# Shifted copies by packed 64-bit adds on GpSimd, and five small operations moved from GpSimd to VectorE

## The chip, the core and the metric

The kernel runs on one core of a Trainium2 chip. A core has engines that run their own instruction streams side by side and meet at semaphores: TensorE (PE; matrix products, which land in PSUM), ScalarE (ACT; functions such as exp), VectorE (DVE; arithmetic along the free axis), GpSimd (POOL; arithmetic between SBUF tensors) and SyncE (SP; issues DMAs). The time is that of one execution on the device, in microseconds (us). 0.2% of this kernel's time is 2.9 us.

## What is computed

Two transformer layers over 2048 tokens of width 512, 32 heads of 16, and an MLP of width 1792. Both layers use the same weights.

```python
def _layernorm(x, axis=-1, eps=1e-5):
    m = jnp.mean(x, axis=axis, keepdims=True)
    v = jnp.var(x, axis=axis, keepdims=True)
    return (x - m) / jnp.sqrt(v + eps)
...
        scores = jnp.einsum("bhqd,bhkd->bhqk", q, k) * (Dh ** -0.5)
        p = _softmax(scores, axis=-1)
        o = jnp.einsum("bhqk,bhkd->bhqd", p, v)
        return (lambda x, *d: x.transpose(*d))(o, 0, 2, 1, 3).reshape(B, S, D) @ wo
...
        h = jnp.einsum("bsd,df->bsf", x, w1) + b1
        h = _gelu(h)
        return jnp.einsum("bsf,fd->bsd", h, w2) + b2
...
    x = x + _A_ref(_layernorm(x, axis=-1), A_wqkv, A_wo)
    x = x + _B_ref(_layernorm(x, axis=-1), B_w1, B_b1, B_w2, B_b2)
    x = x + _A_ref(_layernorm(x, axis=-1), A_wqkv, A_wo)
    x = x + _B_ref(_layernorm(x, axis=-1), B_w1, B_b1, B_w2, B_b2)
```

## The kernel before

**Cells and passes.** The scores of attention are cut into cells of 128 keys by 512 queries of one head (or 256 queries of two heads in the last segments). A pass is one query segment, one group of heads and a range of key tiles; `passes` lists them in order, and a full pass has 16 key tiles by 4 row groups, 64 cells. There are 4096 cells in all. A score matmul uses 32 rows of the PE array, so up to four cells of different row groups run at once (line 1520).

**Two ways through a cell.** An A cell goes to ScalarE: one `activation` takes the exp of two or three cells from PSUM to SBUF (line 2124), and each needs one product with V (17 columns: 16 values and a column of ones that sums the weights). A D cell goes to VectorE. `dfirst` (line 1785) computes `score * E_SCALE + E_BIAS` into uint16; read as bf16, these bits are a piecewise linear approximation of exp. `dchain` then makes three more copies of the plane, shifted by 32, 64 and 96 (128 would be one octave), and the products of the four planes with V and with copies of V scaled by 0.84, 0.71 and 0.59 (`VW`) are summed, so that the errors of the approximation largely cancel. So a D cell needs four products where an A cell needs one. Which key tiles may be D cells is fixed by `KD`: summed over the passes, 1320 of the 4096. A D cell that VectorE has not taken by the end of its pass goes to ScalarE like any other (`next_act`).

**The copies.** Two D cells make a pair (128 x 1024). The first shift, `one` (line 1944), makes plane 1 out of plane 0, on GpSimd where its planned clock is at most `PSHIFT` = 3 us ahead of VectorE's. The second, `two` (line 1969), makes planes 2 and 3 out of 0 and 1 in one VectorE instruction of 128 x 2048; where GpSimd has room it is split into `more` (line 1978, plane 2, GpSimd) and `far` (line 1976, plane 3, VectorE). Scaled copies of V are made by `vcopies` on GpSimd (line 1449), the masked copy of Q for a pass by `qpad` on GpSimd (line 1468; three buffers), the application of the layer norm by `apply` (line 814; GpSimd, or VectorE at the two ends of the kernel), `rstd` by a power on GpSimd (line 800), and the scaling by the softmax sum in `norm` (line 1021; GpSimd for the first six groups of a segment of 512).

**The order.** Nothing is scheduled at run time. `_Sched` simulates the engines while the program is built: each operation is an `_Op` with an engine and a price in us, generators (threads) yield them in order of their data, and at each step the operation that can start first is put at the end of its engine's stream, by priority among those that are ready. Buffers are pools that threads acquire and release. When a group of scores is placed, `attach`, `trade` and `swap` decide from the planned clocks whether D cells join it, and `solo` places a D cell alone. So a price sets not only when work is due but which engine gets it. The planner also keeps GpSimd and VectorE apart where it marks an operation as `port`: a marked VectorE operation is not planned to start inside a GpSimd operation, and a GpSimd operation gives way to a marked one (`GRACE`, `CLOSE`) or waits for it by a semaphore (`op.lock`). When PE would sit idle for longer than a matmul, `fill` puts in a matmul on constants (line 1508); columns that a round of products has no cell for get one too (line 2199).

**Thresholds by piece.** The thresholds of these decisions (`SWAP`, `TOL`, `TAIL` and thirty more, `NAMES`) are read from `ROWS`, 45 rows of values. The cells are divided into 100 pieces, and `PIECES` names for each piece the row that `turn` installs.

Of the kernel before, what the change touches and what calls it, by code (L numbers as in the profile page):

```python
# [9 lines left out]
F16 = mybir.dt.float16  # L10
U16 = mybir.dt.uint16

D = 512
# [113 lines left out]
)  # L127
PIECES = (34, 25, 0, 23, 19, 41, 43, 12, 5, 5, 0, 21, 1, 44, 11, 35, 13, 13, 5, 19, 36, 44, 44, 40, 44, 22, 0, 8, 15, 24, 27, 0, 0, 0, 10, 0, 0, 35,
          14, 0, 0, 32, 18, 31, 38, 0, 22, 22, 22, 30, 0, 29, 14, 16, 16, 40, 0, 6, 44, 39, 26, 0, 4, 30, 16, 0, 23, 19, 0, 42, 44, 15, 15, 23, 23, 0,
          22, 0, 33, 0, 3, 0, 0, 35, 7, 0, 9, 28, 17, 2, 37, 0, 28, 17, 20, 0, 0, 33, 0, 22)  # L130
CLOSE = 0.35
# [6 lines left out]
PMORE = 1  # L138
# [149 lines left out]

# [271 lines left out]
def bass_interleave_layers__mha_block__dense_activation_gelu__prompt_kernel(  # L560
# [15 lines left out]
    with ExitStack() as es:  # L576
# [46 lines left out]
        T["IDENT"] = sb([128, 128], BF16, "ident")  # L623
        T["NHALF"] = sb([128, 4], F32, "nhalf")
# [46 lines left out]
class _Plan:  # L671
# [12 lines left out]
    def init(self):  # L684
# [97 lines left out]
    def ln(self, tiles, dst, dkeys, prio, quick=False, gate=None):  # L782
# [4 lines left out]
        for t in tiles:  # L787
# [3 lines left out]
            if key[0] == "B":  # L791
# [5 lines left out]
        mvk = ["MV.%d" % t for t in tiles]  # L797
        yield _Op("dve", 0.16, lambda e: e.tensor_scalar(T["VARR"][:, sl], T["MV"][:, sl, 1], 1e-5, None, op0=ALU.add),
                  reads=mvk, writes=["VARR.%d" % c])
        yield _Op("pool", 0.37 + 0.18 * n, lambda e: e.tensor_tensor(  # L800
            out=T["RSTD"][:, sl], in0=T["VARR"][:, sl], in1=T["NHALF"][:, 0:n], op=ALU.pow),
            reads=["VARR.%d" % c, "NHALF"], writes=["RSTD.%d" % c])
        yield _Op("dve", 0.157, lambda e: e.scalar_tensor_tensor(
# [7 lines left out]
    def apply(self, c, t, x, quick):  # L811
        T = self.T
        eng, cost = ("dve", 0.4) if quick else ("pool", 0.77)
        return _Op(eng, cost, lambda e: e.tensor_scalar(
            T["XLN"][:, x, :], T["X"][:, t % XT, :], T["RSTD"][:, t:t + 1], T["NMR"][:, t:t + 1], op0=ALU.mult, op1=ALU.add),
            reads=["X.%d" % (t % XT), "RSTD.%d" % c, "NMR.%d" % c], writes=["XLN.%d" % x])
# [165 lines left out]
    def norm(self, l, seg, g, b, part, final):  # L982
# [33 lines left out]
        o = gb % 2  # L1016
        pool = g < 6 and seg[2] == 512
        nb = w // 32
        for i, t in enumerate(ts):
            o3 = T["OTT"][:, o, 0:w].rearrange("p (k c) -> p k c", c=32)[:, :, 16 * t:16 * t + 16]  # L1020
            yield _Op(*(("pool", 0.63 * w / 512) if pool else ("dve", 0.153 + 0.262 * w / 512)), lambda e, i=i, o3=o3: e.tensor_tensor(
                out=o3, in0=x3[:, i * nb:i * nb + nb, 0:16],
                in1=T["RC"][:, i * nb:i * nb + nb, None].to_broadcast([128, nb, 16]), op=ALU.mult),
                reads=["XT", "RC"], writes=["OTT.%d.%d" % (o, t)])
# [405 lines left out]
    def vcopies(self):  # L1430
# [4 lines left out]
        for v in range(len(first)):  # L1435
            l, seg, g, kts = self.pas[first[v]][:4]
            kd = self.kd(first[v])
            js = list(range(len(kd)))
            if js:
                if used[v % 2] is not None:  # L1440
                    yield ("cond", lambda pi=first[used[v % 2] + 1]: self.pv >= pi)
                used[v % 2] = v
                for j in js:
                    yield ("need", ("V", l, kd[j], kd[j] // 4))
                step = kd[1] - kd[0] if len(kd) > 1 else 1
                gb = self.heads(seg, g)[0]
                src = T["V"][l][:, kd[0]:kd[-1] + 1:step, 8 * gb:8 * gb + 8, :].rearrange("p k h c -> p k (h c)")
                for i, w in enumerate(VW):
                    yield _Op("pool", 0.15 + 0.133 * len(js), lambda e, i=i, w=w, v=v, js=js, src=src: e.tensor_scalar(  # L1449
                        T["VC"][:, v % 2, i, js[0]:js[-1] + 1, :], src, w, 1.0, op0=ALU.mult, op1=ALU.mult),  # L1450
                        reads=["V%d.%d" % (l, kt) for kt in kd] + [self.vone(l, kt) for kt in kd], writes=["VC.%d.%d" % (v % 2, i)])
            yield ("give", ("vc", v))
            if not js:
                continue
            self.lend = 1

    def qpad(self):
        T = self.T
        for pi, (l, seg, g, kts, part, final) in enumerate(self.pas):
# [7 lines left out]
            for i, t in enumerate(ts):  # L1467
                yield _Op("pool", 0.27 + 0.42 * w / 512, lambda e, s=s, q=q, i=i, t=t, w=w: e.tensor_scalar(  # L1468
                    T["QP"][:, s, w * i:w * i + w], q, T["MASK"][:, t:t + 1], 1.0, op0=ALU.mult, op1=ALU.mult),
                    reads=["Q.%d.%d" % (b, qc), "MASK"], writes=["QP.%d" % s])  # L1470
# [448 lines left out]
    def dchain(self, pair):  # L1919
# [20 lines left out]
        key = [[self.dkey(pair, i, j) for j in range(n)] for i in range(2)]  # L1940
        u0, u1 = self.planes(pair, 0, n), self.planes(pair, 1, n)
        if self.s.clock["pool"] <= self.s.clock["dve"] + PSHIFT and len(pair["cells"]) == n:
            a, b = u0.rearrange("p j q -> p (j q)"), u1.rearrange("p j q -> p (j q)")
            one = _Op("pool", 0.15 + 0.45 * n, lambda e, a=a, b=b: e.tensor_scalar(b, a, float(SHIFT), 1.0, op0=ALU.add, op1=ALU.mult),  # L1944
                      reads=key[0], writes=key[1])
        else:
            one = _Op("dve", 0.151 + 0.134 * n, lambda e: e.tensor_scalar(u1, u0, SHIFT, None, op0=ALU.add),
                      reads=key[0], writes=key[1])
        one.port = True
        prio = (lambda: UPRIO if any(c[0] <= self.pv and self.left[c[0]] <= URGENT for c in cells) else CPRIO) if URGENT else None  # L1950
        one.prio = prio
        yield one
# [16 lines left out]
        two = _Op("dve", 0.152 + 0.266 * n, lambda e: e.tensor_scalar(  # L1969
            self.planes(sw, 2, n, True), self.planes(sw, 0, n, True), 2 * SHIFT, None, op0=ALU.add),  # L1970
            reads=key[0] + key[1], writes=key[2] + key[3])
        two.port = True
        two.prio = prio
        if one.eng == "pool" and self.s.clock["pool"] <= self.s.clock["dve"] + PMORE and self.room() >= DUMORE:
            a, c, d, b = u0.rearrange("p j q -> p (j q)"), self.planes(pair, 2, n).rearrange("p j q -> p (j q)"), self.planes(pair, 3, n), u1
            far = _Op("dve", 0.151 + 0.134 * n, lambda e: e.tensor_scalar(d, b, 2 * SHIFT, None, op0=ALU.add),
                      reads=key[1], writes=key[3])
            more = _Op("pool", 0.15 + 0.45 * n, lambda e, a=a, c=c: e.tensor_scalar(c, a, float(2 * SHIFT), 1.0, op0=ALU.add, op1=ALU.mult),  # L1978
                       reads=key[0], writes=key[2])
            far.port = more.port = True  # L1980
            far.prio = more.prio = prio
            yield more
            yield far
        else:
            yield two
        if own:
# [3 lines left out]
        for i in range(2 * EARLYP, 4):  # L1990
            self.products(pair, i)

    def units(self, n):
# [313 lines left out]
```

## Time and profile before

| | |
|---|---|
| median of 3 runs | 1451.74 us (1451.57 to 1451.89) |
| profiled execution | span 1450.5 us, first to last instruction; its page gives no other time |
| engines' busy time | PE 1418.4, ACT 1424.3, DVE 1382.8, POOL 995.5 us |
| granted TensorE clock | 1.000 over the span |
| DMA | 55 GB/s in the mean, 19.4% of 16 engines' time |

The granted clock is full, and so it takes no part in what follows. Busy time is the union of the instructions' intervals; on ACT and DVE an instruction's interval overlaps the next one's by some tens to a hundred ns, so that busy time doesn't show very short waits. A row of the groups of instructions has: line, engine, operation, output<-input, shapes, count, then the busy time in us, the mean ns of one, and the idle time of the engine just before them with what ended it. A row of the timeline has the start in us, the length in us, the engine and the instructions.

### The profile page before, as it was taken

What the parts mean: (1) busy time and instruction counts of PE and PEld (TensorE: products, weight loads), DVE (VectorE), ACT (ScalarE), POOL (GpSimd) and SP (SyncE); (2) the same over time, 40 slices, a digit from 0 to 9 for tenths busy, and PEclk for the clock granted to TensorE, in tenths of its full rate; (3) what the DMA queues carried; (4) which work ended last, traced back from release to release, by engine and by line L of the source; (5) the groups of instructions that cost most, each with busy time, mean ns of one, the idle gap of its engine ahead of it and who ended that gap; (6) DMA issues with size and microseconds to landing.
All of it is one profiled execution on the core that took longest, in us unless ns stands there. A gap on an engine that the chain in (4) does not pass through costs nothing.

```text
span 1450.5 us, 45848 instructions
## 1 busy us (share of the span) xinstructions
PE 1418.4 (98%) x19662; PEld 424.7 (29%) x19662; DVE 1382.8 (95%) x2438; ACT 1424.3 (98%) x1406; POOL 995.5 (69%) x1082
## 2 busy tenths in 40 slices
PE   8999999999999999999999999999999999999999
PEld 3222222222222222222222222222222222344445
DVE  7999999999999999999999999999999999999994
ACT  7999999999999999999999999999999999999996
POOL 6676676767776677777676677687767777667751
PEclk9999999999999999999999999999999999999999
DMA  5100001113221133112431123101132203311021
GB/s 159 47 2 2 2 2 38 38 51 97 60 53 31 58 97 89 45 45 72 106 74 38 60 72 91 45 12 36 38 89 67 67 23 96 118 32 39 17 66 41
DMA packets 122166, 80.29 MB, mean 55 GB/s; under 512 B 36717, under 2 KB 120942, under 8 KB 121966
## 3 DMA queue, kind: packets, MB, share of 16 engines
q1 hardware_dynamic: 121966, 77.36, 19.4%
q8 instruction: 158, 2.59, 0.8%
q14 instruction: 42, 0.34, 0.1%
HBM read 65.54 MB, written 4.19 MB: 48 GB/s over the span
## 4 chain that ended last, share of the span: by engine, by line
ACT 42%; PE 41%; DVE 16%; issue 1%; POOL 0%; DMA 0%; DVEq 0%
ACT pt L2124 36%; PE ps L2191 14%; PE ps L1520 14%; PE ps L681 12%; DVE dp L1785 6%; DVE dp L1969 3%; ACT g L1209 2%; ACT kt L2124 1%; DVE g L1188 1%; DVE kt L1785 1%; PE ps L1508 1%; DVE stats L790 1%; ACT q L2124 1%; DVE v L1785 1%; DVE xt L1011 0%
## 5 line engine op out<-in xcount | busy, mean ns | idle before, releaser
L2124 ACT ACTIVATE pt<-ps 128x1024 bf16<-128x1024 f32 (+1 forms) x1264 | 1265.5, 1136 | 4.9 <-PE ps L1520 3.2
L1785 DVE TENSOR_SCALAR dp<-ps 128x512 uint16<-128x512 f32 x931 | 611.5, 681 | 21.5 <-PE ps L1520 18.2
L1944 POOL TENSOR_SCALAR dp<-dp 128x1024 uint16<-128x1024 uint16 (+1 forms) x468 | 490.1, 1056 | 191.0 <-DVE dp L1969 116.7
L1520 PE MATMUL ps<-qp,kt 32*128 32x512 bf16 x4096 | 558.1, 384 | 15.0 <-ACT pt L2124 7.0
L2191 PE MATMUL ps<-dp,vc 128*17 128x512 bf16 (+1 forms) x3120 | 390.2, 359 | 2.3 <-DVE dp L1969 0.9
L2191 PE MATMUL ps<-pt,v 128*17 128x512 bf16 (+1 forms) x3078 | 379.4, 357 | 0.7 <-DVE dp L1969 0.3
L1520 PEld LDWEIGHTS ps<-qp,kt 32*128 32x128 bf16 x4096 | 141.2, 91 | 576.2 <-ACT pt L2124 197.4
L1969 DVE TENSOR_SCALAR dp<-dp 128x2048 uint16<-128x2048 uint16 (+1 forms) x385 | 272.3, 726 | 3.7 <-POOL dp L1944 3.3
L2191 PE MATMUL ps<-dp,v 128*17 128x512 bf16 (+1 forms) x1040 | 149.5, 359 | 3.1 <-DVE xt L1011 1.6
L681 PE MATMUL ps<-xf,wr 128*32 128x512 bf16 (+1 forms) x1888 | 131.7, 365 | 0.4 <-DVE g L1188 0.2
L2191 PEld LDWEIGHTS ps<-dp,vc 128*17 128x17 bf16 x3120 | 98.0, 88 | 102.0 <-issue 58.6
L2191 PEld LDWEIGHTS ps<-pt,v 128*17 128x17 bf16 x3078 | 96.5, 88 | 76.2 <-issue 44.7
L1449 POOL TENSOR_SCALAR vc<-v 128x680 bf16<-128x680 bf16 (+3 forms) x138 | 90.8, 658 | 38.9 <-DVE dp L1969 18.0
L1785 DVE TENSOR_SCALAR kt<-ps 128x512 uint16<-128x512 f32 x154 | 103.6, 682 | 5.1 <-PE ps L1520 4.4
L681 PE MATMUL ps<-wr,g 128*32 128x512 bf16 x1408 | 105.5, 383 | 0.6 <-DVE dp L1785 0.5
L1944 POOL TENSOR_SCALAR kt<-kt 128x1024 uint16<-128x1024 uint16 x77 | 82.1, 1068 | 32.4 <-DVE dp L1969 26.9
L1468 POOL TENSOR_SCALAR qp<-q,mask 128x512 bf16<-128x512 bf16 (+1 forms) x91 | 63.7, 700 | 58.5 <-DVE dp L1969 22.3
L1978 POOL TENSOR_SCALAR dp<-dp 128x1024 uint16<-128x1024 uint16 x83 | 86.6, 1044 | 10.2 <-DVE dp L1969 4.3
L2191 PE MATMUL ps<-kt,vc 128*17 128x512 bf16 (+1 forms) x582 | 88.6, 337 | 0.3 <-DVE kt L1969 0.2
L1188 DVE TENSOR_SCALAR g<-ps,hb1t 128x512 bf16<-128x512 f32 (+1 forms) x112 | 79.3, 708 | 0.7 <-PE ps L681 0.5
L2199 PE MATMUL ps<-b2row,zero 128*17 128x512 bf16 x369 | 78.5, 381 | 0.0
L2191 PE MATMUL ps<-kt,v 128*17 128x512 bf16 (+1 forms) x277 | 57.6, 350 | 0.9 <-DVE dp L1969 0.6
(112 smaller groups left out, 1416.4 us busy)
## 6 DMA issues: line engine op xcount, KB each, us to landing
wr<-in_B_w_dram SPq DMA_DIRECT2D x174, 256.0 KB, 2.9
wr<-in_A_wqkv_dram SPq DMA_DIRECT2D x24, 256.0 KB, 3.1
x<-in_A_x_dram SPq DMA_DIRECT2D x7, 512.0 KB, 4.2
wr<-in_A_wo_dram SPq DMA_DIRECT2D x10, 256.0 KB, 2.9
kept<-x SPq DMA_DIRECT2D x4, 512.0 KB, 2.9
x<-kept SPq DMA_DIRECT2D x4, 512.0 KB, 4.0
out_dram<-x SPq DMA_DIRECT2D x16, 128.0 KB, 1.9
q<-in_B_w_dram SPq DMA_DIRECT2D x3, 512.0 KB, 6.3
```

What stands on the lines that cost most here:

```text
L681: return [lambda e, a=a: e.matmul(out[32 * a:32 * a + 32, :], lhsT=lhsT[:, 32 * a:32 * a + 32], rhs=rhs, start=start, stop=stop, tile_posi ...
L1188: yield _Op("dve", 0.21 + n / 966, lambda e, fc=fc, pb=pb: e.tensor_scalar(T["G"][:, fc, q], pb, T["HB1T"][:, fc:fc + 1], None, op0=ALU.ad ...
L1449: yield _Op("pool", 0.15 + 0.133 * len(js), lambda e, i=i, w=w, v=v, js=js, src=src: e.tensor_scalar(T["VC"][:, v % 2, i, js[0]:js[-1] + 1 ...
L1468: yield _Op("pool", 0.27 + 0.42 * w / 512, lambda e, s=s, q=q, i=i, t=t, w=w: e.tensor_scalar(T["QP"][:, s, w * i:w * i + w], q, T["MASK"] ...
L1520: return (lambda e: e.matmul(o, lhsT=lhsT, rhs=rhs, start=True, stop=True, tile_position=(32 * a, 0)), ["K%d.%d.%d" % (l, gb, kt // 4), "Q ...
L1785: yield _Op("dve", 0.682, lambda e: e.tensor_scalar(u, self.bank(b), E_SCALE, E_BIAS, op0=ALU.mult, op1=ALU.add), reads=["B.%d" % b], writ ...
L1944: one = _Op("pool", 0.15 + 0.45 * n, lambda e, a=a, b=b: e.tensor_scalar(b, a, float(SHIFT), 1.0, op0=ALU.add, op1=ALU.mult), reads=key[0] ...
L1969: two = _Op("dve", 0.152 + 0.266 * n, lambda e: e.tensor_scalar(self.planes(sw, 2, n, True), self.planes(sw, 0, n, True), 2 * SHIFT, None, ...
L1978: more = _Op("pool", 0.15 + 0.45 * n, lambda e, a=a, c=c: e.tensor_scalar(c, a, float(2 * SHIFT), 1.0, op0=ALU.add, op1=ALU.mult), reads=k ...
L2124: yield _Op("act", 0.065 + 0.4267 * n, lambda e, src=src, dst=dst: e.activation(out=dst, in_=src, func=ACT.Exp, scale=0.25), reads=["B.%d" ...
L2191: op.fns.append(lambda e, o=o, lhsT=q[0][0][m], rhs=q[0][1][:, n * m:n * m + n], a=a, st=st, sp=sp: e.matmul(o, lhsT=lhsT, rhs=rhs, start= ...
L2199: op.fns.append(lambda e, o=self.bank(b)[32 * a:32 * a + 17, :], rhs=rhs, a=a, st=not begun[a], sp=end: e.matmul(o, lhsT=T["ZERO"][:, 0:17 ...
```

## The change

1. Shifted copies: `shift` makes both `one` and `two`. On GpSimd it reads four uint16 as one 64-bit integer and adds `by * 32` to each by one `int64_add` with a constant (no value overflows its 16 bits). `one` is 256 words per partition for a pair, `two` 512. `one` goes to GpSimd under the same condition as before; `two` goes there where GpSimd's planned clock is at most `PMORE` = 1 us ahead of VectorE's, else to VectorE as before. The split into `more` and `far` is gone.
2. Five operations go to VectorE: the scaled copies of V, the masked copies of Q, all applications of the layer norm, all scalings by the softmax sum, and `rstd`, which becomes an integer estimate of the inverse root and two correction steps: one power on GpSimd becomes six more VectorE instructions.
3. The planner marks these VectorE operations as `port`, and prices the packed add at 0.18 us and 0.0017 us per word.
4. All 100 pieces use row 0 of `ROWS`.

`KD`, the passes, the priorities and the buffers stay.

```diff
-PIECES = (34, 25, 0, 23, 19, 41, 43, 12, 5, 5, 0, 21, 1, 44, 11, 35, 13, 13, 5, 19, 36, 44, 44, 40, 44, 22, 0, 8, 15, 24, 27, 0, 0, 0, 10, 0, 0, 35,
...
+PIECES = (0,) * 100
...
+PFIX = 0.18
+PWORD = 0.0017
...
+PACKED = SHIFT * 0x0001000100010001
...
+PORTS = ("OTT", "NMR", "RSTD", "RA.", "RY.", "XLN", "VC", "QP")
...
-        self.port = eng == "dve" and self.writes[:1] != [] and self.writes[0].startswith(("OTT", "NMR"))
+        self.port = eng == "dve" and self.writes[:1] != [] and self.writes[0].startswith(PORTS) and not any(k.startswith("B.") for k in self.reads)
...
-        yield _Op("pool", 0.37 + 0.18 * n, lambda e: e.tensor_tensor(
-            out=T["RSTD"][:, sl], in0=T["VARR"][:, sl], in1=T["NHALF"][:, 0:n], op=ALU.pow),
...
+        yield _Op("dve", 0.16, lambda e: e.tensor_scalar(y.bitcast(I32), v.bitcast(I32), -0.5, R_MAGIC, op0=ALU.mult, op1=ALU.add),
+                  reads=vk, writes=yk)
+        for i, (by, less) in enumerate(((1.0, R_LESS), (R_BY * R_BY, 3.0))):
+            yield _Op("dve", 0.16, lambda e: e.tensor_tensor(out=a, in0=y, in1=y, op=ALU.mult), reads=yk, writes=ak)
...
-        eng, cost = ("dve", 0.4) if quick else ("pool", 0.77)
-        return _Op(eng, cost, lambda e: e.tensor_scalar(
+        return _Op("dve", 0.41, lambda e: e.tensor_scalar(
...
-        pool = g < 6 and seg[2] == 512
...
-                    yield _Op("pool", 0.15 + 0.133 * len(js), lambda e, i=i, w=w, v=v, js=js, src=src: e.tensor_scalar(
+                    yield _Op("dve", 0.151 + 0.036 * len(js), lambda e, i=i, w=w, v=v, js=js, src=src: e.tensor_scalar(
...
-                yield _Op("pool", 0.27 + 0.42 * w / 512, lambda e, s=s, q=q, i=i, t=t, w=w: e.tensor_scalar(
+                yield _Op("dve", 0.21 + 0.134 * w / 512, lambda e, s=s, q=q, i=i, t=t, w=w: e.tensor_scalar(
...
+        yield self.shift(sw, 0, 2, n, True, 2, key[0] + key[1], key[2] + key[3], self.s.clock["pool"] <= self.s.clock["dve"] + PMORE)
...
+    def shift(self, pair, i, o, n, both, by, reads, writes, pool):
+        src, dst = self.planes(pair, i, n, both), self.planes(pair, o, n, both)
+        if pool:
+            if both:
+                src, dst = [x.rearrange("p i j q -> p i (j q)").bitcast(U64) for x in (src, dst)]
+            else:
+                src, dst = [x.rearrange("p j q -> p (j q)").bitcast(U64) for x in (src, dst)]
+            op = _Op("pool", PFIX + PWORD * 128 * n * (1 + both), lambda e: e.int64_add(dst, src, by * PACKED), reads=reads, writes=writes)
+        else:
+            op = _Op("dve", 0.151 + 0.134 * n * (1 + both), lambda e: e.tensor_scalar(dst, src, by * SHIFT, None, op0=ALU.add), reads=reads, writes=writes)
+        op.port = True
+        return op
```

More of the change, by code (lines that the diff above doesn't have):

```diff
@@ L11 @@
 U16 = mybir.dt.uint16
+I32 = mybir.dt.int32
+U64 = mybir.dt.uint64
 D = 512
@@ L168 @@
 SHIFT = 32
+PACKED = SHIFT * 0x0001000100010001
+R_BY = 0.703952253
+R_LESS = 2.38924456
+R_MAGIC = float(0x5F1FFFF9)
+R_SCALE = 4.0 / (R_BY * R_BY)
 VW = (0.83984375, 0.70703125, 0.59375)
+PORTS = ("OTT", "NMR", "RSTD", "RA.", "RY.", "XLN", "VC", "QP")
 ENG_SEM = {"pe": "pe", "act": "act", "dve": "dve", "pool": "pool"}
@@ L797, in ln @@
         mvk = ["MV.%d" % t for t in tiles]
-        yield _Op("dve", 0.16, lambda e: e.tensor_scalar(T["VARR"][:, sl], T["MV"][:, sl, 1], 1e-5, None, op0=ALU.add),
-                  reads=mvk, writes=["VARR.%d" % c])
-        yield _Op("pool", 0.37 + 0.18 * n, lambda e: e.tensor_tensor(
-            out=T["RSTD"][:, sl], in0=T["VARR"][:, sl], in1=T["NHALF"][:, 0:n], op=ALU.pow),
-            reads=["VARR.%d" % c, "NHALF"], writes=["RSTD.%d" % c])
+        v, y, a = T["VARR"][:, sl], T["RY"][:, sl], T["RA"][:, sl]
+        vk, yk, ak = ["VARR.%d" % c], ["RY.%d" % c], ["RA.%d" % c]
+        yield _Op("dve", 0.16, lambda e: e.tensor_scalar(v, T["MV"][:, sl, 1], 1e-5, R_SCALE, op0=ALU.add, op1=ALU.mult),
+                  reads=mvk, writes=vk)
+        yield _Op("dve", 0.16, lambda e: e.tensor_scalar(y.bitcast(I32), v.bitcast(I32), -0.5, R_MAGIC, op0=ALU.mult, op1=ALU.add),
+                  reads=vk, writes=yk)
+        for i, (by, less) in enumerate(((1.0, R_LESS), (R_BY * R_BY, 3.0))):
+            yield _Op("dve", 0.16, lambda e: e.tensor_tensor(out=a, in0=y, in1=y, op=ALU.mult), reads=yk, writes=ak)
+            yield _Op("dve", 0.16, lambda e, by=by: e.scalar_tensor_tensor(out=a, in0=a, scalar=by, in1=v, op0=ALU.mult, op1=ALU.mult),
+                      reads=ak + vk, writes=ak)
+            out, ok = (T["RSTD"][:, sl], ["RSTD.%d" % c]) if i else (y, yk)
+            yield _Op("dve", 0.16, lambda e, less=less, out=out: e.scalar_tensor_tensor(
+                out=out, in0=a, scalar=less, in1=y, op0=ALU.subtract, op1=ALU.mult), reads=ak + yk, writes=ok)
         yield _Op("dve", 0.157, lambda e: e.scalar_tensor_tensor(
@@ L1940, in dchain @@
         key = [[self.dkey(pair, i, j) for j in range(n)] for i in range(2)]
[L1941 to L1951, printed above, removed]
+        one = self.shift(pair, 0, 1, n, False, 1, key[0], key[1], self.s.clock["pool"] <= self.s.clock["dve"] + PSHIFT)
         yield one
@@ L1968, in dchain @@
         key += [[self.dkey(pair, i, j) for j in range(n)] for i in (2, 3)]
[L1969 to L1985, printed above, removed]
+        yield self.shift(sw, 0, 2, n, True, 2, key[0] + key[1], key[2] + key[3], self.s.clock["pool"] <= self.s.clock["dve"] + PMORE)
         if own:
```

12 lines of the change are left out of this document (5 added, 7 removed).

## The prediction

> **What bounds the kernel now.** I read first the page's busy times and the chain that ended last, then the groups of instructions with their shapes kept apart, the waits, and a stretch of the timeline.
>
> ```profile
> span 1450.5 us, 45848 instructions
> ...
> PE 1418.4 (98%) x19662; PEld 424.7 (29%) x19662; DVE 1382.8 (95%) x2438; ACT 1424.3 (98%) x1406; POOL 995.5 (69%) x1082
> ...
> ACT 42%; PE 41%; DVE 16%; issue 1%; POOL 0%; DMA 0%; DVEq 0%
> ACT pt L2124 36%; PE ps L2191 14%; PE ps L1520 14%; PE ps L681 12%; DVE dp L1785 6%; DVE dp L1969 3%; ACT g L1209 2%; ACT kt L2124 1%; DVE g L1188 1%; DVE kt L1785 1%; PE ps L1508 1%; DVE stats L790 1%; ACT q L2124 1%; DVE v L1785 1%; DVE xt L1011 0%
> ...
> L1520 PE MATMUL ps<-qp,kt 32*128 32x512 bf16 x4096 | 558.1, 384 | 15.0 <-ACT pt L2124 7.0
> ```
>
> The chain is shared by ACT (42%) and PE (41%), both busy for 98%; VectorE has 16% of it, GpSimd none. ACT's part is the exp of A cells, so only fewer A cells shorten it. The last row has the 4096 cells; the next ones say who takes them.
>
> ```profile
> L2124 ACT ACTIVATE pt<-ps 128x1024 bf16<-128x1024 f32 x1050 | 997.5, 1062 | 2.5 <-PE ps L1520 1.5
> ...
> L1785 DVE TENSOR_SCALAR dp<-ps 128x512 uint16<-128x512 f32 x931 | 611.5, 681 | 21.5 <-PE ps L1520 18.2
> ...
> L2124 ACT ACTIVATE pt<-ps 128x1536 bf16<-128x1536 f32 x214 | 309.7, 1499 | 2.4 <-PE ps L1520 1.7
> ...
> L1785 DVE TENSOR_SCALAR kt<-ps 128x512 uint16<-128x512 f32 x154 | 103.6, 682 | 5.1 <-PE ps L1520 4.4
> ...
> L1785 DVE TENSOR_SCALAR v<-ps 128x512 uint16<-128x512 f32 x80 | 53.5, 681 | 2.5 <-PE ps L1520 2.0
> ```
>
> VectorE takes 931 + 154 + 80 = 1165 D cells, ACT 2931 A cells. An A cell costs ACT 997.5 / 2100 = 0.475 us. `KD` allows 1320 D cells, so 155 that might have been VectorE's went to ACT. VectorE is 95% busy: that may be why.
>
> PE's 98% hides some slack, which stands in its fillers:
>
> ```profile
> L1508 PE MATMUL ps<-b2row 128*32 128x512 bf16 x444 | 36.0, 384 | 1.2 <-DVE dp L1785 0.6 <-DVE kt L1785 0.5
> ...
> L1508 PE MATMUL ps<-b2row,zero 128*17 128x512 bf16 x144 | 12.2, 383 | 0.0
> ```
>
> 36.0 + 12.2 = 48.2 us are matmuls on constants, put where PE would have waited. Their busy tenths by slice of the span:
>
> ```profile
> busy tenths in 40 slices 2223403020700100002200103299030040053000
> ```
>
> They crowd into a dozen slices; where the digit is 0, PE has no slack.
>
> **The change part by part.** *GpSimd's copies.* The trace has no 64-bit add. The nearest rows are today's shifts:
>
> ```profile
> L1944 POOL TENSOR_SCALAR dp<-dp 128x1024 uint16<-128x1024 uint16 x463 | 487.0, 1061 | 189.3 <-DVE dp L1969 115.1 <-DVE dp L1976 15.4 <-DVE dp L1785 14.9
> ...
> L1944 POOL TENSOR_SCALAR dp<-dp 128x512 uint16<-128x512 uint16 x5 | 3.2, 639 | 1.7 <-DVE dp L1969 1.6
> ```
>
> (1061 - 639) / 512 = 0.82 ns for an element, and 0.22 us fixed. A 64-bit word takes at least the slot of one element, at most four of them (then nothing is packed). `one` has 256 words, `two` 512: with one slot 0.43 + 0.64 = 1.07 us for a pair, with two 0.64 + 1.06 = 1.70, with four 1.06 + 1.90 = 2.96. I take two slots, a word being two 32-bit halves, which is also near the price that the change writes down (0.62 + 1.05). [...]
>
> With 1281 D cells (below) there are 640 pairs: 1088 us (bounds 685 and 1894). What leaves GpSimd:
>
> ```profile
> L1449 POOL TENSOR_SCALAR vc<-v 128x680 bf16<-128x680 bf16 (+3 forms) x138 | 90.8, 658 | 38.9 <-DVE dp L1969 18.0
> L1468 POOL TENSOR_SCALAR qp<-q,mask 128x512 bf16<-128x512 bf16 (+1 forms) x91 | 63.7, 700 | 58.5 <-DVE dp L1969 22.3
> ...
> L1978 POOL TENSOR_SCALAR dp<-dp 128x1024 uint16<-128x1024 uint16 x83 | 86.6, 1044 | 10.2 <-DVE dp L1969 4.3 <-DVE dp L1976 2.1 <-DVE kt L1976 1.7
> L814 POOL TENSOR_SCALAR xln<-x,rstd,nmr 128x512 bf16<-128x512 bf16 x58 | 44.3, 770 | 20.5 <-DVE dp L1969 13.7 <-DVE dp L1976 3.0 <-DVE v L1969 1.6
> L1021 POOL TENSOR_TENSOR ott<-xt,rc 128x256 bf16<-128x256 f32 x42 | 28.6, 680 | 29.0 <-DVE dp L1969 21.0 <-DVE dp L1976 3.1 <-DVE kt L1969 2.4
> L800 POOL TENSOR_TENSOR rstd<-varr,nhalf 128x4 f32<-128x4 f32 x10 | 11.1, 1110 | 6.1 <-DVE dp L1969 4.7 <-DVE dp L1976 1.0 <-DVE varr L798 0.3
> L800 POOL TENSOR_TENSOR rstd<-varr,nhalf 128x2 f32<-128x2 f32 x11 | 9.8, 887 | 9.6 <-DVE dp L1969 6.4 <-DVE dp L1976 1.8 <-DVE v L1969 0.7
> ```
>
> All of it goes; the packed adds alone remain, 1088 of some 1430 us (76%, today 69%). Off the path, as today, while a pair stays under the 2.2 us named below.
>
> *VectorE.* It loses `two` and `far` and gains the five operations. Rows, with the nearest ones for what isn't there yet:
>
> ```profile
> L1969 DVE TENSOR_SCALAR dp<-dp 128x2048 uint16<-128x2048 uint16 x380 | 270.6, 731 | 3.7 <-POOL dp L1944 3.3
> L1969 DVE TENSOR_SCALAR kt<-kt 128x2048 uint16<-128x2048 uint16 x45 | 33.3, 741 | 0.0
> L1969 DVE TENSOR_SCALAR v<-v 128x2048 uint16<-128x2048 uint16 x25 | 17.6, 709 | 0.0
> ...
> L1976 DVE TENSOR_SCALAR dp<-dp 128x1024 uint16<-128x1024 uint16 x83 | 38.3, 464 | 0.0
> L1976 DVE TENSOR_SCALAR kt<-kt 128x1024 uint16<-128x1024 uint16 x32 | 13.8, 434 | 0.0
> L1976 DVE TENSOR_SCALAR v<-v 128x1024 uint16<-128x1024 uint16 x15 | 7.3, 483 | 0.0
> ...
> L814 DVE TENSOR_SCALAR xln<-x,rstd,nmr 128x512 bf16<-128x512 bf16 x6 | 2.3, 412 | 0.3
> L1021 DVE TENSOR_TENSOR ott<-xt,rc 128x256 bf16<-128x256 f32 x14 | 6.3, 451 | 0.1
> L803 DVE SCALAR_TENSOR_TENSOR nmr<-mv,rstd 128x2 f32<-128x2 f32 x11 | 1.7, 157 | 0.1
> ```
>
> Loss: 270.6 + 33.3 + 17.6 + 38.3 + 13.8 + 7.3 = 381 us. Gain: 731 and 464 ns make 0.26 ns per element and 0.20 us fixed, so 138 V copies of at most 680 elements cost 0.37 each (52 us); 91 Q copies at the 412 ns of line 814 (37); 58 layer norms at 412 (24); 42 scalings at 451 (19); 23 x 6 small steps for `rstd` at 157 (22). Together 154 us (the sizes are known; a third more is 205, and overlap with the next instruction makes it less). Net -227 us, so VectorE falls from 1383 to 1156 us before it takes more cells. If every third `two` comes back to VectorE because GpSimd's planned clock is ahead, that is 213 x 0.731 = 156 us, and the relief is 71.
>
> At nothing I cost the later results of the moved operations: Q and V copies are made passes ahead, into three and two buffers. The `rstd` chain is bare at the end of the kernel; there six steps of 157 ns replace a trip to GpSimd of about the same 0.9 us, so 0, within half a us either way.
>
> *The new wait.* Planes 2 and 3 now wait behind GpSimd's queue, so the products on them come later, and while the next pair's `one` stands behind a `two`, its products do too. PE has A products to put in meanwhile; without that cover, a 1.06 us `two` replaces a 0.73 us one, 0.33 us for each pair that PE stands waiting for.
>
> *More D cells.* Bounds 0 and 155; I take three quarters, 116, since 227 us would pay for 333 evacuations of 0.681 and the cells a pass leaves at its end are lost in any case. VectorE: 1156 + 79 = 1235 us. ACT: -116 x 0.475 = -55 us (0 to -74).
>
> *PE.* A D cell has three products more, an A cell fewer saves part of a score step. Steps of PE:
>
> ```profile
> 703.12 0.39 PE L2191 MATMUL ps<-dp,v 128*17 128x512 bf16 x4
> 703.33 0.39 PE L2191 MATMUL ps<-dp,vc 128*17 128x512 bf16 x4
> ...
> 703.87 0.39 PE L1520 MATMUL ps<-qp,kt 32*128 32x512 bf16 x3
> ...
> 704.19 0.39 PE L2191 MATMUL ps<-dp,vc 128*17 128x512 bf16 x4
> ```
>
> Four products start 0.21 us after four others; after a score step the next comes 0.32 later. 116 x 3 / 4 x 0.21 = +18 us; 116 / 2.17 cells per exp (2742 in 1264) x 0.32 = -17. So +1, and PE gains only from fewer waits: 0 to -48 us of fillers. I take half, -24, since they crowd into stretches that are short of work for other reasons.
>
> *Row 0 for all pieces.* No row of the trace has the price of a threshold. ACT's visible idle time is 1450.5 - 1424.3 = 26 us: I let it double (+26), with bounds of none left (-26) and three times as much (+52).
>
> **Sum**, against the span: by ACT 1450.5 - 55 + 26 = 1421.5; by PE 1450.5 + 1 - 24 = 1427.5. The later one ends it; with the 1.2 us by which the median exceeds the span, 1429 us. Bounds of the two: all fillers gone, 1450.5 + 2 - 48 + 1.2 = 1405; no more D cells and +52, 1504.
>
> **Rivals.** *1, slower: the thresholds.* They decide when a D cell joins a group of scores. If row 0 fits the new prices badly, PE waits for banks, in the slices that have no filler now. For it: PE stands at no slack there, and the pace of MLP and projections was set for other prices. Against: 227 us of room on VectorE. It decides once fillers grow instead of shrinking; half as many again, +24, is 1476.
>
> *2, slower: the port.*
>
> ```profile
> 700.98 1.29 DVE L1969 TENSOR_SCALAR dp<-dp 128x2048 uint16<-128x2048 uint16 x2
> ...
> 701.75 1.42 POOL L1944 TENSOR_SCALAR dp<-dp 128x1024 uint16<-128x1024 uint16 x1 [1.76 <-DVE dp L1969]
> ...
> 705.20 1.04 POOL L1944 TENSOR_SCALAR v<-v 128x1024 uint16<-128x1024 uint16 x1 [2.04 <-DVE v L1785]
> ...
> PEld ps L1520 <- DVE dp L1785: 126.4, 290, 0.9
> POOL dp L1944 <- DVE dp L1969: 116.7, 115, 3.0
> ```
>
> A shift that began under a `two` took 1.42 us where a free one took 1.04, and GpSimd stood 116.7 us for `two`: the engines hinder each other. If 467 new VectorE operations (138 + 91 + 58 + 42 + 138) each meet a packed add in 76% of cases and lose half of its 0.85 us, that is 151 us, VectorE is back at 1386, no cell moves, evacuations queue behind the waiting copy, and PE waits for those already (126.4 us): 1450.5 + 26 + 1.2 = 1478. Against: today's port time, 995 + 381, is more than 1088 + 154, and the planner holds a marked operation until GpSimd is done and gives VectorE other work. [...]
>
> *3, slower by far: no packing on the chip.* GpSimd then needs 1894 us while the planner counts on 1.70 a pair: about 1900. It decides from 1429 / 640 = 2.2 us a pair.
>
> *4, no change: VectorE wasn't what kept cells away,* but banks: 1451.
>
> *5, more:* all fillers go: 1405.
>
> **Chances.** Forecast 0.55 (own range 1412 to 1446), rivals 0.17, 0.08, 0.04, 0.08, 0.08. Range: 1403 to 1474, which leaves out rival 3 and parts of 1, 2 and 5. A measurement tells 0.2% (2.9 us) from nothing. Faster: the forecast, rival 5, half of 4 and a little of 1, 0.70; same 0.05; slower 0.25.
>
> **What would show it.** Packed adds of about 0.64 and 1.06 us on GpSimd, 70 to 80% busy; VectorE near 1235 us or 87%; some 1280 evacuations on line 1785's successor; exps on ACT down from 2931 cells to some 2815; fillers near 24 us. Wrong if D cells stay near 1165, if VectorE's copies last far beyond 0.4 us, or if PE's fillers or ACT's waits grow.

## The result and the profile after

| | before | after |
|---|---|---|
| median | 1451.82 us (4 runs beside the changed kernel) | 1473.80 us (4 runs, 1473.71 to 1475.09) |
| ratio, 95% interval | | 1.0153 (1.0139 to 1.0167) |
| span of the profiled execution | 1450.5 us | 1472.0 us |
| D cells taken by VectorE | 1165 | 1179 |
| fillers of PE | 48.2 us | 55.8 us |

The kernel became slower by 22.0 us. The page of the changed kernel, with busy times first and then the chain that ended last:

```profile
span 1472.0 us, 46013 instructions
...
PE 1421.7 (97%) x19695; PEld 427.4 (29%) x19695; DVE 1234.8 (84%) x2377; ACT 1420.5 (97%) x1368; POOL 949.2 (64%) x1178
...
PE 57%; ACT 29%; DVE 13%; issue 1%; POOL 1%; POOLq 0%; DVEq 0%; ACTq 0%
```

VectorE lost 148 us of busy time, GpSimd 46 us, and PE and ACT, which the end hangs on, nothing: PE has 3.3 us more and ACT 3.8 less. The groups of instructions, shapes kept apart, say what VectorE did with its room:

```profile
L1799 DVE TENSOR_SCALAR dp<-ps 128x512 uint16<-128x512 f32 x890 | 594.2, 684 | 86.2 <-PE ps L1534 79.0
L1799 DVE TENSOR_SCALAR kt<-ps 128x512 uint16<-128x512 f32 x189 | 128.2, 684 | 37.6 <-PE ps L1534 36.6
...
L1799 DVE TENSOR_SCALAR v<-ps 128x512 uint16<-128x512 f32 x100 | 68.1, 686 | 16.2 <-PE ps L1534 14.8 <-PE ps L2192 0.6
...
L1522 PE MATMUL ps<-b2row 128*32 128x512 bf16 x452 | 35.5, 384 | 1.0 <-DVE dp L1799 0.5 <-DVE kt L1799 0.3
...
L1522 PE MATMUL ps<-b2row,zero 128*17 128x512 bf16 x240 | 20.3, 383 | 0.0
```

It took 890 + 189 + 100 = 1179 D cells, 14 more than before, where 116 were reckoned with. Ahead of these evacuations it now stands idle for 86.2 + 37.6 + 16.2 = 140 us, nearly all of it for PE's scores; before, the same three idle times were 21.5 + 5.1 + 2.5 = 29 us. So VectorE has its room and waits for scores. PE's fillers grew by 7.6 us to 35.5 + 20.3 = 55.8, where they were to halve.

PE has a second kind of matmuls on constants, those for a column that a round of products has no cell for. They became fewer; the kernel before:

```profile
L2199 PE MATMUL ps<-b2row,zero 128*17 128x512 bf16 x369 | 78.5, 381 | 0.0
```

and the changed one:

```profile
L2200 PE MATMUL ps<-b2row,zero 128*17 128x512 bf16 x223 | 53.0, 381 | 0.0
```

They run beside products (in the kernel before two of them start at 700.74 and 700.75 us, a product at 700.74), so their time is not idle time of PE; what they show is the number of rounds. With 2931 + 4 x 1165 = 7591 products before and 2917 + 4 x 1179 = 7633 after, four columns to a round, it is 1990 rounds before and 1964 after; at 0.21 us a round that is some 5.5 us less, an estimate.

A loss of another kind stands in the opening. The timeline of the changed kernel, GpSimd's first instructions and its first packed adds, and ACT's first exp:

```profile
0.73 0.20 POOL L699 MEMSET ident<- 128x128 bf16 x1 [0.29 <-POOLq L2293]
8.54 0.28 POOL L700 TENSOR_SCALAR_AFFINE_SELECT ident<-ident 128x128 bf16<-128x128 bf16 x1 [7.60 <-issue]
...
18.93 2.37 ACT L2125 ACTIVATE pt<-ps 128x1536 bf16<-128x1536 f32 x2 [1.26 <-PE ps L1534]
...
40.82 0.61 POOL L1988 INT64_ADD dp<-dp  x1 [28.39 <-DVE dp L1799]
41.99 1.04 POOL L1988 INT64_ADD dp<-dp  x1 [0.56 <-DVE xln L829]
```

and the same two places in the kernel before:

```profile
1.17 0.29 POOL L691 TENSOR_SCALAR_AFFINE_SELECT ident<-ident 128x128 bf16<-128x128 bf16 x1 [0.24 <-POOL ident L690]
...
11.35 2.37 ACT L2124 ACTIVATE pt<-ps 128x1536 bf16<-128x1536 f32 x2 [1.28 <-PE ps L1520]
```

GpSimd stands for 7.60 us ahead of its affine select, with nothing in the profile that releases it, and the first exp comes 7.58 us later. In the kernel before, which has no packed add, the same instruction starts after 0.24 us. No view shows what GpSimd does in the 7.60 us; whether packed adds bring them is what e3 and e5 ask.

The packed adds themselves last 0.61 us (256 words) and 1.04 us (512 words).

### The profile page after: what moved, and what is told of

Read it like the earlier page. It is cut to its first block, busy times and chain, and to the rows that moved or that the text cites. A ratio compares the mean times of both kernels' runs of the same rounds, so it can differ in the third digit from the quotient of the medians.

```text
span 1472.0 us, 46013 instructions
## 1 busy us (share of the span) xinstructions
PE 1421.7 (97%) x19695; PEld 427.4 (29%) x19695; DVE 1234.8 (84%) x2377; ACT 1420.5 (97%) x1368; POOL 949.2 (64%) x1178
## 4 chain that ended last, share of the span: by engine, by line
PE 57%; ACT 29%; DVE 13%; issue 1%; POOL 1%; POOLq 0%; DVEq 0%; ACTq 0%
ACT pt L2125 22%; PE ps L2192 20%; PE ps L1534 19%; PE ps L690 16%; DVE dp L1799 5%; ACT g L1223 3%; ACT kt L2125 2%; DVE kt L1799 1%; DVE vc L1463 1%; PE ps L1522 1%; DVE xt L1026 1%; ACT L2125 1%; ACT L1223 1%; POOL dp L1988 1%; DVE v L1799 1%
## 5 line engine op out<-in xcount | busy, mean ns | idle before, releaser
L2125 ACT ACTIVATE pt<-ps 128x1024 bf16<-128x1024 f32 (+1 forms) x1137 | 1178.9, 1164 | 19.8 <-PE ps L1534 16.3
L1988 POOL INT64_ADD dp<-dp x880 | 714.5, 819 | 353.3 <-DVE dp L1799 144.1
L1799 DVE TENSOR_SCALAR dp<-ps 128x512 uint16<-128x512 f32 x890 | 594.2, 684 | 86.2 <-PE ps L1534 79.0
L2192 PE MATMUL ps<-dp,vc 128*17 128x512 bf16 (+1 forms) x3009 | 325.8, 357 | 1.0 <-ACT pt L2125 0.5
L2192 PE MATMUL ps<-pt,v 128*17 128x512 bf16 (+1 forms) x2838 | 296.3, 359 | 4.6 <-ACT pt L2125 1.9
L1988 POOL INT64_ADD kt<-kt x186 | 151.6, 816 | 86.3 <-DVE kt L1799 50.8
L1799 DVE TENSOR_SCALAR kt<-ps 128x512 uint16<-128x512 f32 x189 | 128.2, 684 | 37.6 <-PE ps L1534 36.6
L1988 POOL INT64_ADD v<-v x98 | 80.4, 822 | 42.9 <-DVE v L1799 24.5
L1799 DVE TENSOR_SCALAR v<-ps 128x512 uint16<-128x512 f32 x100 | 68.1, 686 | 16.2 <-PE ps L1534 14.8
L2125 ACT ACTIVATE kt<-ps 128x1024 bf16<-128x1024 f32 (+1 forms) x78 | 78.9, 1097 | 0.0
L2192 PE MATMUL ps<-v,vc 128*17 128x512 bf16 x300 | 63.6, 381 | 0.2 <-POOL v L1988 0.2
L2125 ACT ACTIVATE v<-ps 128x1024 bf16<-128x1024 f32 (+1 forms) x54 | 56.0, 1113 | 1.6 <-PE ps L2192 0.8
```

Source lines behind the costliest of these rows:

```text
L1799: yield _Op("dve", 0.682, lambda e: e.tensor_scalar(u, self.bank(b), E_SCALE, E_BIAS, op0=ALU.mult, op1=ALU.add), reads=["B.%d" % b], writ ...
L1988: op = _Op("pool", PFIX + PWORD * 128 * n * (1 + both), lambda e: e.int64_add(dst, src, by * PACKED), reads=reads, writes=writes)
L2125: yield _Op("act", 0.065 + 0.4267 * n, lambda e, src=src, dst=dst: e.activation(out=dst, in_=src, func=ACT.Exp, scale=0.25), reads=["B.%d" ...
L2192: op.fns.append(lambda e, o=o, lhsT=q[0][0][m], rhs=q[0][1][:, n * m:n * m + n], a=a, st=st, sp=sp: e.matmul(o, lhsT=lhsT, rhs=rhs, start= ...
```

## The experiments

Each ratio is against runs of the kernel before on the same chip (medians 1451.99 to 1452.56 us).

| experiment | starts from | median us (runs) | ratio (95%) |
|---|---|---|---|
| e1_row0 | before | 1476.97 (4) | 1.0168 (1.0153 to 1.0183) |
| e2_two_back | after | 1509.89 (4) | 1.0393 (1.0377 to 1.0408) |
| e3_one_library | after | 1467.28 (4) | 1.0103 (1.0086 to 1.0120) |
| e4_old_table | after | 1471.96 (4) | 1.0134 (1.0119 to 1.0149) |
| e5_scaling_back | after | 1973.39 (1) | single run, no interval |
| e6_more_planes | e3 | 1468.57 (4) | 1.0114 (1.0099 to 1.0129) |
| e7_unmarked | e3 | 1506.92 (4) | 1.0383 (1.0364 to 1.0401) |
| e8_less_pe | e3 | 1442.53 (4) | 0.9934 (0.9921 to 0.9948) |
| e9_less_act | e3 | 1436.61 (4) | 0.9892 (0.9879 to 0.9906) |
| e10_new_table | e3 | 1442.34 (5) | 0.9935 (0.9921 to 0.9949) |

**The table alone (e1) and the old table in the changed kernel (e4).**

```diff
 e1, in the kernel before:
-PIECES = (34, 25, 0, 23, 19, 41, ...
+PIECES = (0,) * 100
 e4, in the changed kernel:
-PIECES = (0,) * 100
+PIECES = (34, 25, 0, 23, 19, 41, ...
```

> The kernel before with one edit: all 100 pieces use row 0 of the thresholds; every operation stays where it was. Theory (the loss of the change is mostly the table of thresholds): slower, about 1476 us, 24 us over before, since the planner's own end moves from 1442 to 1466 us and VectorE takes 1114 D cells for 1165. Rival (the loss comes from the moved operations and the port, the table is worth nothing): within 4 us of 1452.

> The changed kernel with the old table of thresholds by piece. Theory (the table is worth something only with the prices it belongs to; the planner's end is 1454 against 1453): 1474 to 1478, no gain. Rival (the table's thresholds are better in themselves, so that the change lost 24 us by dropping it): about 1450.

The kernel before, with nothing changed but the table, loses 1476.97 - 1452.40 = 24.6 us. Its groups show the two kinds of fillers:

```profile
L1506 PE MATMUL ps<-b2row 128*32 128x512 bf16 x440 | 37.2, 394 | 0.2
...
L1506 PE MATMUL ps<-b2row,zero 128*17 128x512 bf16 x328 | 28.1, 383 | 0.0
```

They grew from 48.2 to 37.2 + 28.1 = 65.3 us, and its D cells fell to 894 + 149 + 71 = 1114. Its page has the busy times and the chain:

```profile
PE 1437.4 (97%) x19832; PEld 432.2 (29%) x19832; DVE 1353.3 (92%) x2362; ACT 1445.8 (98%) x1391; POOL 996.4 (67%) x1091
...
ACT 60%; PE 30%; DVE 7%; POOL 1%; issue 1%; DMA 0%; ACTq 0%
```

PE has 19.0 us more than before, and ACT 21.5, near the 51 x 0.475 = 24 us of the cells that came back to it. So rows by piece were worth 24.6 us there. But the same table is worth only 1473.80 - 1471.96 = 1.8 us in the changed kernel, by the ratios 0.0019 of 1452, 2.8 us, which the two intervals do not tell from nothing. It is a fit to one set of prices and does not carry over.

**The second shift (e2).**

```diff
-        yield self.shift(sw, 0, 2, n, True, 2, key[0] + key[1], key[2] + key[3], self.s.clock["pool"] <= self.s.clock["dve"] + PMORE)
+        yield self.shift(sw, 0, 2, n, True, 2, key[0] + key[1], key[2] + key[3], False)
```

> The changed kernel with the second shift always on VectorE; the first one is still a packed add and the five operations are still on VectorE. Theory (the packed second shift is what gains, some 29 us in the planner's reckoning, 1453 to 1482): about 1502 us. Rival (VectorE is not what limits, so it can carry the second shift too): within 5 us of the changed kernel's 1474.

The page, busy times and chain:

```profile
PE 1445.5 (96%) x19893; PEld 432.7 (29%) x19893; DVE 1438.9 (96%) x2836; ACT 1454.8 (97%) x1395; POOL 362.8 (24%) x568
...
DVE 44%; ACT 27%; PE 27%; issue 1%; POOL 0%; DMA 0%; POOLq 0%; DVEq 0%
```

With `two` back on VectorE and the five operations there as well, VectorE is 96% busy and has 44% of the chain, GpSimd is at 24%. The packed second shift is worth 1509.9 - 1473.8 = 36.1 us. Most of that pays for the five operations: from row 0 in the kernel before (1477.0) to here is +32.9 us, some 7 of them the opening's (7.41 us ahead of the affine select in e2), so the five operations, with the packed first shift, cost some 26 us, and some 10 are left.

**A packed add in the opening (e3).** A packed add of 0 ahead of the affine select, on data that it leaves as it is:

```diff
         yield _Op("pool", 0.1, lambda e: e.memset(T["IDENT"][:], 0.0), writes=["IDENT"])
+        yield _Op("pool", 0.25, lambda e: e.int64_add(T["IDENT"][:].bitcast(U64), T["IDENT"][:].bitcast(U64), 0), reads=["IDENT"], writes=["IDENT"])
         yield _Op("pool", 0.3, lambda e: e.affine_select(
```

> [...] Rival (the opening is hidden by slack later): 1474. [...]

The timeline of the opening:

```profile
1.08 0.24 POOL L700 INT64_ADD ident<-ident  x1
1.48 0.29 POOL L701 TENSOR_SCALAR_AFFINE_SELECT ident<-ident 128x128 bf16<-128x128 bf16 x1 [0.17 <-POOL ident L700]
...
12.28 2.37 ACT L2126 ACTIVATE pt<-ps 128x1536 bf16<-128x1536 f32 x2 [1.27 <-PE ps L1535]
```

The stand ahead of the affine select is 0.17 us in place of 7.60, the first exp comes 6.65 us earlier, and the time falls by 1473.80 - 1467.28 = 6.5 us (7.3 by the ratios) with the same 1179 D cells. It was bare time on the path, and no slack later hid it.

**One of the five operations left on GpSimd (e5).** The scaling by the softmax sum, 42 instructions, goes back.

```diff
+        pool = g < 6 and seg[2] == 512
...
-            yield _Op("dve", 0.153 + 0.262 * w / 512, lambda e, i=i, o3=o3: e.tensor_tensor(
+            yield _Op(*(("pool", 0.63 * w / 512) if pool else ("dve", 0.153 + 0.262 * w / 512)), lambda e, i=i, o3=o3: e.tensor_tensor(
```

> The changed kernel with one of the five operations undone: the scaling by the softmax sum is on GpSimd again (42 instructions). [...] Rival (the 7.6 us are paid once in a program, and the five operations were moved for GpSimd's time alone): about 1466, as the planner's end is 1444 against 1453.

GpSimd's waits (line, what it waited for, us in all, times, longest):

```profile
POOL ott L1036 <- issue: 245.0, 34, 7.9
POOL dp L1989 <- issue: 201.8, 34, 6.4
...
POOL kt L1989 <- issue: 24.1, 4, 6.3
```

245.0 + 201.8 + 24.1 = 471 us of GpSimd standing with nothing that releases it: some 7.2 us ahead of a scaling and 5.9 ahead of the packed add that follows. The chain:

```profile
PE 52%; issue 18%; ACT 14%; DVE 11%; POOL 5%; POOLq 0%; DVEq 0%; ACTq 0%
```

The kernel lost 1973.4 - 1473.8 = 500 us, and 18% of its chain, some 355 us, is such standing, where the changed kernel has 1%. (Over this execution the granted clock of TensorE was 0.865, and PE was busy for 1528.3 us in place of 1421.7, which has a part too.) So a scaling between two packed adds brings such a stand on either side, some 13 us for the two, and this move of the change belongs to its packing. Whether the other four do is not tested. Not every instruction of GpSimd pays: the affine select of e3 follows a packed add after 0.17 us.

**More room for D cells (e6).** If buffers keep cells from VectorE, more of them should let it take cells: 20 planes in place of 16, ten sets of buffers in place of eight, paid for by fewer exp buffers.

```diff
-PT_RING = 30
+PT_RING = 22
...
-SETS = 8
-NPL = 16
+SETS = 10
+NPL = 20
```

> The kernel of e3 with 20 planes for D cells in place of 16, 10 sets in place of 8 and 22 buffers for exps in place of 30; VectorE then takes 1228 D cells for 1179, ScalarE 2868 A cells for 2917. The prediction's premise (fewer A cells shorten it, 0.475 us each on ScalarE): 23 us faster than e3, about 1444. Theory (PE is the bound: three products more for a D cell, and its waits stay): no faster than e3, about 1472 by the planner's end of 1458 against 1453.

```profile
PE 1422.2 (97%) x19798; PEld 428.5 (29%) x19798; DVE 1255.1 (86%) x2414; ACT 1399.0 (95%) x1375; POOL 1001.0 (68%) x1237
```

These are its busy times. VectorE took 955 + 181 + 92 = 1228 cells, 49 more than in e3, and ACT fell from 1420.4 to 1399.0 us, near the 49 x 0.475 = 23 us that the cells are worth; PE stayed at 1422 us. The time went by 1.3 us the other way, which the intervals do not tell from nothing. More D cells alone are not time here; whether the eight exp buffers that paid for them cost something is not separated. The 49 cells are 49 of the 1320 - 1179 = 141 that `KD` allows and ACT still had, so too few planes and sets were one of the things that kept cells away.

**The port (e7).** The planner's marks of the moved operations are taken away, so that it plans them into GpSimd's instructions.

```diff
-PORTS = ("OTT", "NMR", "RSTD", "RA.", "RY.", "XLN", "VC", "QP")
+PORTS = ("OTT", "NMR")
```

> The kernel of e3 with the planner's port mark taken off the operations that the change moved (only the scaling and the mean's term keep it); the same instructions on the same engines, planned as if GpSimd and they could overlap. Theory A (the two engines do hinder each other there, and the mark is needed): the planner's end falls by 14 us to 1439, the chip gives none of it, 1467 or more, and Q copies, V copies and packed adds take longer than 0.34, 0.49 and 0.61 or 1.04 us. Theory B (the mark costs more than the collisions): about 1453.

Three groups of the changed kernel, where the marks hold, and the same three of e7:

```profile
L1988 POOL INT64_ADD dp<-dp x880 | 714.5, 819 | 353.3 <-DVE dp L1799 144.1 <-DVE qp L1482 42.2 <-PE ps L2192 39.3
...
L1482 DVE TENSOR_SCALAR qp<-q,mask 128x512 bf16<-128x512 bf16 x75 | 25.7, 343 | 7.5 <-PE ps L1534 7.3
...
L829 DVE TENSOR_SCALAR xln<-x,rstd,nmr 128x512 bf16<-128x512 bf16 x64 | 25.5, 418 | 0.5
```

```profile
L1989 POOL INT64_ADD dp<-dp x883 | 721.1, 823 | 385.7 <-DVE dp L1800 243.8 <-PE ps L2193 48.6 <-DVE ott L1036 36.5
...
L830 DVE TENSOR_SCALAR xln<-x,rstd,nmr 128x512 bf16<-128x512 bf16 x64 | 41.8, 674 | 0.3
...
L1483 DVE TENSOR_SCALAR qp<-q,mask 128x512 bf16<-128x512 bf16 x75 | 37.1, 496 | 5.6 <-PE ps L1535 5.0
```

A layer norm goes from 418 to 674 ns and a Q copy from 343 to 496, and the time rises by 39.6 us over e3, although the planner's own end is 14 us earlier. The packed add keeps its price (819 and 823 ns in the mean), so it is VectorE's instruction that takes longer; a packed add that does is not seen in these means, and what holds the VectorE instruction is not shown. With the marks this cost isn't paid: e3 has 418 and 345 ns. Not all of the 39.6 us need come from there: the granted clock was 0.983 to 0.992 in the four runs of e7 and 0.999 to 1.000 in those of e3, and its part is not separated.

**Which engine sets the end (e8, e9).** Work is left out: on PE half of the first MLP product, on ACT the gelu of six blocks of seven.

```diff
 e8:
-                fns += self.quads(pb, T["WR"][w][:, o:o + 128], T["XF"][:, dc, q], dc == 0, dc == NDC - 1)
-            for h in range(0, 4, FQ):
+                fns += self.quads(pb, T["WR"][w][:, o:o + 128], T["XF"][:, dc, q], dc == 0, dc == 1)
+            for h in range(0, 2, FQ):
 e9:
-            yield _Op("act", 0.065 + 0.4267 * half * n / 512 + ...
+            g = T["G"][:, f:f + 1, seg[1]:seg[1] + n]...
+            yield _Op("act", 0.065 + 0.4267 * n / 512 + ...
```

> The kernel of e3 without half of the first MLP product (two of its four blocks of 128 rows are left out), some 236 steps of 0.21 us on PE, 50 us; everything else is planned anew. If PE alone is the bound: about 50 us faster than e3's 1467, 1417. If ACT alone is: 1467. If both set the end in turn (the planner's end goes from 1453 to 1427): about 1442.

> The kernel of e3 without most of the gelu (one of seven blocks of 512 columns in each instruction is left), 14 x 2.56 + 2 x 1.3 = 38 us less on ScalarE. If ACT alone is the bound: about 1429. If PE alone is: 1467. If both set the end in turn (the planner's end goes from 1453 to 1426): about 1440.

Some 50 us less of PE's work gave 24.8 us against e3, and some 38 us less of ACT's gave 30.7. The busy times of e8:

```profile
PE 1394.5 (97%) x18930; PEld 410.8 (29%) x18930; DVE 1228.6 (85%) x2389; ACT 1411.6 (98%) x1361; POOL 966.4 (67%) x1201
```

and of e9:

```profile
PE 1399.0 (97%) x19496; PEld 422.5 (29%) x19496; DVE 1219.6 (85%) x2354; ACT 1387.2 (97%) x1379; POOL 938.7 (65%) x1164
```

Against e3 (PE 1421.7, ACT 1420.4, 1179 D cells) both fell each time: in e8 PE by 27 us and ACT by 9, with 1195 D cells; in e9 ACT by 33 and PE by 23, with 1161 D cells and 12 us fewer fillers. Neither engine sets the end alone, and work that the order moves between A and D cells evens them out.

**A table for the new prices (e10).** The same 45 rows; a row for each piece chosen so that the planner's own end is early. Its row for the first pieces is (11, 0, 0, 24, 41, 17, 20, 0, 24, 7, ...).

```diff
-PIECES = (0,) * 100
+PIECES = (11, 0, 0, 24, 41, 17, 20, 0, 24, 7, ...
```

> The kernel of e3 with a table of thresholds by piece chosen for the new prices from the same 45 rows, by the planner's own end (1430 in place of 1453 us, 1192 D cells for 1179, fillers 36 for 51 us). Theory (the change itself gains some 10 us, and dropping the table hid it): about 1445 us, faster than before's 1452 by 0.5%. Rival (the planner's gain is fitted to its own model and the chip gives none of it): 1460 to 1467.

Busy times, chain and fillers:

```profile
PE 1404.9 (97%) x19471; PEld 420.0 (29%) x19471; DVE 1238.2 (86%) x2387; ACT 1413.0 (98%) x1383; POOL 962.7 (67%) x1192
...
ACT 47%; PE 41%; DVE 10%; issue 1%; POOL 0%; DMA 0%; POOLq 0%; ACTq 0%; DVEq 0%
```

```profile
L1523 PE MATMUL ps<-b2row 128*32 128x512 bf16 x264 | 22.4, 384 | 1.6 <-DVE dp L1800 1.2
...
L1523 PE MATMUL ps<-b2row,zero 128*17 128x512 bf16 x188 | 17.4, 383 | 0.0
```

The table brings 1467.3 - 1442.3 = 24.9 us, as much as the old one did in the kernel before, and this version beats both kernels: 0.9935 of the time before. Fillers are 22.4 + 17.4 = 39.8 us. VectorE still has only 884 + 208 + 100 = 1192 D cells and 14% of its time idle.

## Why the prediction was wrong

**The account.** With one table for both, row 0, the kernel before takes 1477.0 us (e1) and the changed one without the stand in its opening 1467.3 (e3): parts 1 to 3 of the change gain 9.7 us. With a table fitted to each, 1452.4 and 1442.3: they gain 10.1 (how much better either fit could be is not known). What the change as made lost is the fit of the table, +24.6, and the stand in the opening, +6.5: 24.6 - 9.7 + 6.5 = 21.4, from 1452.4 to 1473.8. The D cells go the same way: row 0 takes 51 away (1165 to 1114), parts 1 to 3 bring 65 (1114 to 1179), and 14 are left of it.

**The step that failed first: "Row 0 for all pieces".** Its price was near, +26 against a measured 24.6, but it went into the sum of ACT alone, while PE's sum (1427.5), which had no term for it, ended the forecast. The thresholds act on PE too: in e1 it was busy for 19.0 us more, its fillers grew by 17.1 us, and in the changed kernel by 7.6. With 24.6, PE's own sum would have been 1427.5 + 24.6 = 1452 us before anything else. On ACT the size was right by luck: it was meant as idle time, which grew in e1 only from 26 to 1476.8 - 1445.8 = 31 us; the rest was work, the 51 cells that came back. Rival 1 put the thresholds on PE, where they were missing. That its 1476 is near the measured 1473.8 is luck in part: it let the fillers grow by 24 us, they grew by 7.6, and the stand in the opening and the gain of parts 1 to 3, which nearly cancel, are not in it. It got 0.17, and the one reason set against it, "227 us of room on VectorE", did not hold: the room was there, and PE's fillers grew all the same. Its words "fits the new prices badly" are only half right: no table at hand fitted them, the old one neither (e4), and one that was fitted gave the 24.9 us back (e10).

**"More D cells", -55 us on ACT.** With the 14 cells that came, ACT's own sum would have been 1450.5 - 7 + 26 = 1470 and not 1421.5, so correcting the first step alone would not have been enough. The premise was the half sentence "VectorE is 95% busy: that may be why" cells go to ACT. It is right in part: with one table for both, 65 cells come over, with fitted ones 27. But with VectorE 84% busy 141 of the 1320 still go to ACT. Why is counted while the order is planned, where a D cell is to join a group of scores (`attach`, `trade`; a cell may be refused several times, and `solo`, which also asks for VectorE's clock, is not counted):

```
                          before   after
VectorE's clock too late      13       7
no free planes               188     166
no free bank in PSUM        1111    1032
```

In these places VectorE's lateness is almost never the reason. And where cells did come over, they were worth far less than 0.475 us each: from e1 to e3 65 cells took 25.4 us off ACT and the time fell by 9.7; in e6 49 cells took 21 us off ACT and the time did not fall, since PE did not follow. In e8 and e9, which gained, both fell. Rival 4 named banks as what keeps the cells away; most refusals counted here are for banks, but in e6 more planes and sets brought 49 cells over, and its time left out the table and the stand in the opening.

**"PE gains only from fewer waits", -24.** The direction holds for parts 1 to 3, the size was twice too large: fillers fall from 65.3 (e1) to 55.8 at row 0 and from 48.2 to 39.8 (e10) with fitted tables, 8 to 10 us each time, next to the measured gain of 10. At row 0 the rounds of products fell too, from 1992 to 1964 (530 and 223 constants at lines 2197 and 2200 beside 2982 + 4 x 1114 and 2917 + 4 x 1179 products), some 6 us by the same estimate; fillers and rounds together are near the 15.7 us by which PE's busy time fell from e1 to e3.

**What was left out.** The 7.60 us ahead of the affine select had no term in the sum. The rows of before could not show them, since that kernel has no packed add and stands for 0.24 us there.

**What was right.** The packed adds: 0.64 and 1.06 forecast, 0.61 and 1.04 measured, (1.04 - 0.61) / 256 = 1.7 ns a word, about two of the 0.82 ns of an element, so rival 3 is dead, and GpSimd's 949 us are less than 1088 mostly since fewer pairs came. VectorE's busy time of 1235 us came out to the figure, but by luck, as two errors cancel: 102 cells fewer than reckoned are 69 us less work, and the relief was 69 us smaller. The groups added up show that the work was counted fairly well, 1525.2 us before and 1339.6 after, a fall of 186 us where 227, less 10 for the 14 cells, were reckoned with (of the 31 missing, 14 are 20 second shifts that stayed on VectorE and some 13 `rstd`, which has seven instructions more in place of six and takes 35 us in place of 22); the other 38 are that VectorE's intervals overlap by 142 us before and by 105 after, so that its busy time falls by 148 only. The moved copies were counted well too: the V copies are 486 ns long where all 680 columns are copied, against 0.37 us forecast, but with the short ones the 138 of them have 52.6 us against 52.

**Rival 2, the port,** was a real cost (39.6 us in e7, the clock's part included, against 26 in its sum), but the planner's marks prevent it, as the prediction's "against" had it.

**What stays open.** The planner's own end was 1442.2 us for the kernel before (measured 9.6 later), 1452.8 for the changed one and for e3 (measured 21.0 and 14.5 later). So 10.6 of the 22 us were in the planned order, 6.5 are the stand in the opening, and some 5 us come from a place that no run here tells apart. By the planned ends in the expectations, e1 came 11 us after its plan and e10 12. What the refused cells' banks are held by is not shown either.

## What to carry to other kernels

An engine at 95% is no bound until a wait says so: before costing its relief, look for who waits for it, and ask what stands in the way once it is free; here VectorE waited for scores, and 148 us less of its busy time were worth 10. Thresholds that were fitted to one set of prices are part of the kernel's time (24.6 us here): whoever changes prices must fit them again before judging the change, and a comparison without that judges the table. Where a new kind of instruction comes to GpSimd, look through its whole stream, from the first instruction on, for idle time that nothing in the profile releases: here 7.60 us ahead of the affine select, 6.5 of them in the kernel's time, and 471 us where scalings stood between packed adds (e5).

## What was not expected of the hardware

- In programs with packed adds GpSimd stood idle at some places with nothing in the profile that released it: 7.60 us ahead of the affine select in the opening of the changed kernel, which a packed add ahead of it took away (0.17 us in e3), and in e5 7.2 us in the mean ahead of a scaling and 5.9 us ahead of the packed add after it, 471 us over 72 places.
- A 64-bit add with a constant handles four uint16 in a word: 512 words take 1.04 us, where the ordinary shift of 1024 elements of the kernel before took 1.06: twice the elements in the same time.
- Where VectorE is planned into a packed add, it is VectorE's instruction that grows (418 to 674 ns for a layer norm), and the packed add's price does not change.
